# Linear attention with an MLP behind it: first batch's diagonal sums by matrix products, v's odd heads exchanged on chip, 16-bit sign copy, one wide product of U and x

## The chip, the cores and the metric

The kernel runs on one core of a Trainium2 chip. The metric is device microseconds of one execution, the median over several runs. A profile of one execution gives each engine's instructions: TensorE (PE; its weight loads are shown apart as PEld), VectorE (DVE), ScalarE (ACT), GpSimd (POOL) and SyncE (SP), the last of which here only issues DMAs; ACT issues a few too.

## The reference

Two stages, one behind the other. The first is an attention with a decaying state, over B = 4 batches, H = 8 heads, S = 768 positions and D = 48 channels; the second is a low-rank mixing over positions and an MLP.

```python
for t in range(S):
    kt, vt, rt = (k[:, :, t], v[:, :, t], r[:, :, t])
    cur = np.einsum('bhd,bhe->bhde', u[None] * kt, vt)
    y[:, :, t] = np.einsum('bhd,bhde->bhe', rt, state + cur)
    state = w[None, :, :, None] * state + np.einsum('bhd,bhe->bhde', kt, vt)
...
x = y.transpose(0, 2, 1, 3).reshape(B, S, H * D)          # 384 channels
h = x.transpose(0, 2, 1) @ U @ V                          # rank 32
u_ = x + h.transpose(0, 2, 1)
out = u_ + np.maximum(u_ @ w_ch1, 0.0) @ w_ch2            # 384 -> 1536 -> 384
```

The term with u touches only position t itself: it gives v[t] times the number sum over d of r[t,d] u[d] k[t,d], one number for each head and position. These are the diagonal sums. U, V, w_ch1 and w_ch2 come as 64-bit floats, r, k, v, w and u as 32-bit ones.

## The kernel before

**Attention.** Each batch is cut into six chunks of 128 positions (NCH = 6; chunk n counts on over the batches, and `front(n)` is true for the first batch's six). A chunk has two halves of 64 positions and four pairs of heads. Tables of powers of w turn the decay into scaled copies of r and k: `tables` makes them at the start, `tab` among them, which ACT copies from PSUM (L462) once PE has turned it (L460). For a chunk, `a_load` brings r, k and v (L618), and `a_load_odd` brings the odd heads of v a second time, with the two halves of positions exchanged, as `vsw` (L630): TensorE needs an operand's rows to stand where the other operand's rows stand. `a_ks` multiplies k by `tab` (L662), with a memset of the padding columns on POOL (L661). `a_tr` turns r and the scaled k on TensorE (ptr and ptk, L712) and writes rT and kT (L721, L727, L733). `a_part` issues the products: scores (L751), state updates (L766), scores times v (L787), state times r (L793). One chunk's two parts each carry the scores of the next chunk in turn with their own products.

**Diagonal sums.** `a_dv` multiplies r by k (L669) and by u (L671), for the first batch's chunks 1 to 5 on POOL, chunk 0 on whichever of POOL and DVE the planner picks; u lies in `ub`, broadcast to all partitions (L416). `a_dg` sums over d on DVE (L677) and multiplies v by the sums, eight small ACT products in the first batch (L681). `a_x` adds this to the chunk's result (L892).

**Weights.** `weight_units` has 27 units: U, two of V, 12 of w_ch1, 12 of w_ch2 (128 x 384 values each). A unit's 64-bit values become 32-bit floats in four steps: one byte of the low word to a 3-bit number (L518 on DVE or L522 on ACT), a scaling of the high word on ACT (L534), the sign taken over from the high word (L525, DVE), and a shift and join (L528, DVE). A weight is then split into a rounded value (L548, ACT) and the rest (L549, DVE or POOL).

**From attention to MLP.** `c_gx` multiplies U with a chunk's x (three products of 128 columns, L938; they stand in the bank named wake); `c_g0` takes the sum (L947, L948); `c_x` and `c_xu` turn x and add the mixing; then `m_1` and `m_2` are the MLP, in blocks of 384 positions, each hidden tile followed by ACT (L1080) and DVE (L1081). The second to fourth batch's attention runs between the MLP products of the batch before. TensorE's calls through the helper `whole` all show as L344.

**Order.** Nothing is issued in the order of the text. Every step is put in a list with a key (`at(t, ...)`), and a planner, `Plan.schedule`, goes through the operations with an estimated duration each, gives each to one of the engines that it may run on (`one_of`, `on_either`), and fixes the order of each engine's queue. A smaller key goes first among operations that are ready. On the chip every queue keeps that order, and waits where an estimate was wrong. Where the planner sees PE idle before the first batch's U products are done, it puts in products of the identity with itself (wake), which nobody reads. Buffers with a tag (`xbuf`, `wbuf`, `bank`) are rings; the bank ring "acc" has three PSUM banks.

Of the kernel before, what the change touches and what calls it, by code (L numbers as in the profile page):

```python
# [275 lines left out]
def dve(n):  # L276
    return 130 + 1.09 * n


def act(n):  # L280
    return 285 + 0.6 * n
# [7 lines left out]
def rwkv_moe(ctx: ExitStack, tc: tile.TileContext, r, k, v, w, u, U, V, w1, w2, out):  # L289
# [33 lines left out]
    def cbuf(shape, dt, name):  # L323
        return Buf(const, shape, dt, None, 1, name)
# [61 lines left out]

    wT = cbuf([PD, NP, 1], F32, "wT")
    ub = cbuf([128, H, D], F32, "ub")
    flag = cbuf([1, 1], I32, "flag")

    tabT = cbuf([PD, 2, NP, C2 + 2], F32, "tabT")
# [14 lines left out]
            awake.append(bank_)  # L406
        return fn

    def load_w():
        dma(lambda q: q.dma_start(wT.t[:HP, :, 0], bass.AP(tensor=w.tensor, offset=w.offset, ap=[[1, HP], [2 * D, NP]])),  # L410
            [(wT, 0)], [], HP * NP, 4, ns=730)
        dma(lambda q: q.dma_start(wT.t[HP:, :, 0], bass.AP(tensor=w.tensor, offset=w.offset + D, ap=[[1, D], [2 * D, NP]])),
            [(wT, 1)], [], D * NP, 4, ns=580)

    def load_ub():
        dma(lambda q: q.dma_start(ub.t, u.rearrange("h d -> (h d)").partition_broadcast(128)), [ub], [], 128, 1536, ns=650)  # L416
# [70 lines left out]
    def unit(name, shape, parts, split):  # L487

        P_ = shape[0]
        n = 1  # L490
        for s_ in shape[1:]:
            n *= s_
        raw = big([128, 2 * n], I32, f"raw_{name}") if wide else big([128, n], F32, f"raw_{name}")

        def view(ap):
            return ap if len(shape) == 2 else ap.rearrange("p (a c) -> p a c", a=shape[1])

        loaded = [(raw, i) for i in range(len(parts))]
# [12 lines left out]
        def fl():  # L511
            return view(word(0).bitcast(F32) if wide else raw.t[:P_])

        def on_dve_byte():
            nc.vector.tensor_scalar(word(0), byte(), 2.0 ** -5, 7.0, ALU.mult, ALU.min)  # L518

        def on_act_byte():  # L520

            nc.scalar.activation(word(0), byte(), AF.Copy, scale=7.49 / 255)  # L522

        def sign():
            nc.vector.scalar_tensor_tensor(word(0), word(1), -2 ** 31, word(0), ALU.bitwise_and, ALU.bitwise_or)  # L525

        def join():
            nc.vector.scalar_tensor_tensor(word(0), word(1), 3, word(0), ALU.logical_shift_left, ALU.bitwise_or)  # L528

        def convert():  # L530
            if wide:
                op("DVE", 100 + 0.65 * n, on_dve_byte, [(raw, "lo")], loaded, lock=True,
                   alt=[("ACT", act(n) + 100, on_act_byte, False)])
                on_act(n, lambda: nc.scalar.activation(word(1).bitcast(F32), word(1).bitcast(F32), AF.Copy,  # L534
                                                       scale=2.0 ** -112), [(raw, "hi")], loaded)
                op("DVE", dve(n), sign, [(raw, "lo")], [(raw, "hi")], lock=True)
                op("DVE", dve(n), join, [(raw, "lo")], [(raw, "hi")], lock=True)
            split(fl, raw)
        return load, convert
# [45 lines left out]
    def front(n):  # L585

        return n < NCH
# [5 lines left out]
    def a_load(n):  # L593
        b, c = divmod(n, NCH)
        if n < 4:
            t3 = xbuf([128, 2 * H * HP + DM], F32, "uTl" if n % 2 else "uTh", 2, f"ld_{n}")

            def part(i):
                if i < 2:
                    return t3.t[:, i * H * HP:(i + 1) * H * HP].rearrange("p (h d) -> p h d", h=H)  # L600
                return t3.t[:, 2 * H * HP:].rearrange("p (h d) -> p h d", h=H)
            ts = [(t3, i) for i in range(3)]
        else:
            t3 = [wbuf([128, H, D if i == 2 else HP], F32, ("ldr", "ldk", "ldv")[i], (NR, NR, 3)[i],
                       f"ld{'rkv'[i]}_{n}") for i in range(3)]

            def part(i):
                return t3[i].t
            ts = t3
        if turned(n) and not front(n):  # L610
            for i in range(2):
                op("POOL", 250, lambda i=i: nc.gpsimd.memset(part(i)[:, :, D:], 0.0), [(ts[i], f"pad{i}")], [])
        if front(n):
            for i in range(2):
                on_dve(32, lambda e, i=i: e.memset(part(i)[:, :, D:], 0.0), [(ts[i] if n >= 4 else t3, f"pad{i}")], [])
        for i, src in enumerate((r, k, v)):
            eng = "ACT" if n < 3 and i == 1 else "SP"
            dma(lambda q, i=i, src=src: q.dma_start(part(i)[:, :, :D], src[b, :, c * C:(c + 1) * C, :].rearrange("h p d -> p h d")),  # L618
                [ts[i] if n < 4 else (t3, i)] if n < 4 else [(ts[i], "d")], [], 1024, 192, eng=eng)
        rs[n], ks_[n], vs[n] = [((lambda i=i: part(i)), ([(t3, i), (t3, f"pad{i}")] if n < 4 else [(ts[i], "d"), (ts[i], f"pad{i}")])) for i in range(3)]  # L620
        if n < 4 or not front(n):
            a_load_odd(n)

    def a_load_odd(n, dk=0.0):

        b, c = divmod(n, NCH)
        t = (xbuf([128, NP, D], F32, "x", NX, f"vsw_{n}") if front(n) else wbuf([128, NP, D], F32, "vsw", 3, f"vsw_{n}"))
        for i in range(2):
            s0 = c * C + i * C2
            dma(lambda q, i=i, s0=s0: q.dma_start(t.t[(1 - i) * C2:(2 - i) * C2],  # L630
                                                  v[b, 1::2, s0:s0 + C2, :].rearrange("h p d -> p h d")),
                [(t, i)], [], 256, 192, ns=610, eng="ACT" if n < 3 else "SP", dk=dk)
        vsw[n] = t

    bls = {}

# [26 lines left out]
                  only="DVE" if front(n) else None)  # L663

    def a_dv(n):
        (rt, rb), (kt, kb) = rs[n], ks_[n]
        dv = dvs[n] = (xbuf([128, H, D], F32, "hh", NH, f"dv_{n}") if front(n) else
                       wbuf([128, H, D], F32, "dv", 2, f"dv_{n}"))
        on_either(384, lambda e: e.tensor_mul(dv.t, rt()[:, :, :D], kt()[:, :, :D]), [dv], rb + kb,  # L669
                  only="POOL" if front(n) and n else None)  # L670
        on_either(384, lambda e: e.tensor_mul(dv.t, dv.t, ub.t), [dv], [ub], only="POOL" if front(n) and n else None)  # L671

    def a_dg(n):
        dv = dvs[n]
        vt, vb = vs[n]
        dg = dgs[n] = wbuf([128, H], F32, "dg", 2, f"dg_{n}")
# [2 lines left out]
        def small(h0=0, h1=H):  # L679
            for h in range(h0, h1):  # L680
                nc.scalar.activation(dv.t[:, h], vt()[:, h], AF.Copy, scale=dg.t[:, h:h + 1])  # L681
        if front(n):
            for h in range(0, H, 2):
                op("ACT", 560, lambda h=h: small(h, h + 2), [(dv, h)], vb + [dg])
            return
# [248 lines left out]

    def c_gx(n):

        for i in range(3):
            o = pe(225, lambda i=i: whole(wk.t[:3 * R, 128 * (i + 1):128 * (i + 2)], lhsT=Uf.t[:, n].rearrange("p k r -> p (k r)"),  # L938
                                      rhs=xs[n].t[:, 128 * i:128 * (i + 1)], start=False, stop=n == NCH - 1,
                                      skip_group_check=True), [(wk, "g")], [Uf, xs[n]])  # L940
        return o

    def c_g0():
        def pt():
# [278 lines left out]
    at(-100, load_w)  # L1223
    at(-99, lambda: a_load(0))
    at(-98, load_ub)
    at(-97, tables)
    for n in range(1, NCH):
        at(-90 + n, lambda n=n: a_load(n))
    wu = weight_units()
# [9 lines left out]
    for i, (load, convert) in enumerate(wu):  # L1239

        at(-84.9 + 0.01 * i if i < 3 else -50 + 0.1 * i if i < 20 else T0 + 2 * (i - 20), load)
        at(T0 + (use[i] * PER if i > 2 else -14) - 6 + 0.01 * i, convert)

    def prepare(n, t):
        fs = [lambda: a_ks(n), lambda: a_tr(n, 1), lambda: a_tr(n, 0), lambda: a_dv(n)]
        for i, f in enumerate(fs[1:3] + fs[:1] + fs[3:] if n == 0 else fs):
            at(t + 0.2 * i, f)

    def attention(b, t0, per, lead, step):
        n0 = b * NCH  # L1250
        for c in range(NCH):
# [4 lines left out]
                at(t - 1, lambda n=n: a_first(n))  # L1256
            at(t, lambda n=n: a_part(n, 0))
            at(t + per / 2, lambda n=n: a_part(n, 1))
            if front(n + 4):

                at(t + per / 2 + 0.01, lambda n=n: a_load_odd(n + 4, -100.0))
            at(t - 0.1, lambda n=n: a_dg(n))
            if b == 0:
                at(max(t + per - 0.05, 27.0 + 0.1 * c), lambda n=n: gx.append(c_gx(n)))
# [80 lines left out]
```

## Time and profile before

| What | Value |
|---|---|
| median of 3 runs | 438.04 us (437.14 to 439.49) |
| profiled execution | 439.95 us |
| its span, first to last instruction | 437.9 us |
| mean granted TensorE clock | 0.984 |
| busy share PE, PEld, DVE, ACT, POOL | 96%, 91%, 61%, 33%, 13% |
| first product of the MLP | 56.20 us from the span's start |
| DMA | 43.93 MB, 100 GB/s on average |

How the profile is read: a row of a timeline gives start, duration, engine, line, operation, the tiles by name (output <- inputs) and the shapes; what stands in brackets is the time for which the engine was idle before, and what released it. A row of a group gives the count, the busy time, the mean of one in ns, and the idle time before them. Engines overlap their own neighbouring instructions by some tens of ns, so two starts can lie closer than a duration. The granted clock is the share of full speed that TensorE was given.

### The profile page before, as it was taken

The numbers are of one execution on the slowest core, as the hardware profiler recorded it, in microseconds if no ns is written. First come the engines' busy times: TensorE is split into PE (matmuls) and PEld (weight loads), VectorE is DVE, ScalarE is ACT, GpSimd is POOL, SyncE is SP. The second block draws the span as 40 slices with busy tenths as digits, with TensorE's granted clock in tenths as the row PEclk, the third lists the DMA queues.
The fourth block names the chain that finished last, engine by engine and source line by source line (L and its number), as shares of the span: only waits on it lengthen the run. The fifth ranks groups of instructions, "written<-read, shape, count | busy, mean of one in ns | idle before, by whom it ended". The sixth has DMA issues, their size and how long they took to land.

```text
span 437.9 us, 12193 instructions
## 1 busy us (share of the span) xinstructions
PE 419.4 (96%) x5125; PEld 399.8 (91%) x5125; DVE 267.8 (61%) x602; ACT 142.9 (33%) x399; POOL 55.6 (13%) x92
## 2 busy tenths in 40 slices
PE   8889999999999999999999999999999999999991
PEld 8678899889999999999999999999999999999991
DVE  6979699999887757767775456567522351122121
ACT  1679679934421213121112221222112131111110
POOL 2651151223110002011100001101100000000000
PEclk9989699999999999999999999999999999999998
DMA  9979999654466876744586653231100510001001
GB/s 145 162 162 340 335 199 222 103 84 83 81 88 139 148 146 117 136 87 76 105 168 102 96 147 56 48 64 30 55 2 1 98 65 1 0 0 55 1 0 61
DMA packets 178975, 43.93 MB, mean 100 GB/s; under 512 B 168993, under 2 KB 175650, under 8 KB 178914
## 3 DMA queue, kind: packets, MB, share of 16 engines
q1 hardware_dynamic: 174162, 42.20, 46.9%
q10 hardware_dynamic: 4752, 0.89, 1.5%
q8 instruction: 42, 0.69, 0.7%
q14 instruction: 19, 0.16, 0.1%
HBM read 36.57 MB, written 6.49 MB: 98 GB/s over the span
## 4 chain that ended last, share of the span: by engine, by line
PE 81%; DVE 8%; ACT 3%; DMA 3%; POOL 1%; issue 1%; SPq 0%; ACTq 0%; DVEq 0%; POOLq 0%
PE p L344 64%; PE pav L787 5%; PE pav L793 4%; PE pu L344 3%; DVE raw_w L528 2%; DVE raw_w L525 2%; PE pab L751 2%; DMA ld<-in_r_dram 1%; DMA ld<-in_v_dram 1%; PE pab L766 1%; PE wake L344 1%; DVE hl L1081 1%; PE pG L958 1%; ACT dv L681 1%; POOL dv L671 1%
## 5 line engine op out<-in xcount | busy, mean ns | idle before, releaser
L344 PE MATMUL p<-uTh,w1s 128*128 128x384 f32 x576 | 148.2, 338 | 0.0
L1081 DVE SCALAR_TENSOR_TENSOR hl<-p,hh 128x384 fp32r<-128x384 f32 x96 | 53.2, 554 | 119.3 <-ACT hh L1080 119.0
L344 PE MATMUL p<-w2s,hh 128*128 128x384 f32 x576 | 120.3, 340 | 0.6 <-ACT hh L1080 0.6
L1080 ACT ACTIVATE hh<-p 128x384 fp32r<-128x384 f32 x96 | 47.2, 491 | 210.3 <-PE p L344 208.7
L344 PEld LDWEIGHTS p<-uTh,w1s 128*128 128x128 f32 x576 | 102.9, 188 | 0.8
L344 PEld LDWEIGHTS p<-w2s,hh 128*128 128x128 f32 x576 | 99.8, 188 | 2.8 <-ACT hh L1080 0.9
L344 PE MATMUL p<-uTl,w1s 128*128 128x384 f32 x288 | 96.4, 335 | 0.0
L344 PE MATMUL p<-w2s,hl 128*128 128x384 f32 x288 | 65.8, 335 | 0.0
L344 PEld LDWEIGHTS p<-uTl,w1s 128*128 128x128 f32 x288 | 54.0, 188 | 0.0
L344 PEld LDWEIGHTS p<-w2s,hl 128*128 128x128 f32 x288 | 51.4, 188 | 0.0
L787 PE MATMUL pav<-vsw,am 64*64 64x48 f32 x384 | 33.0, 226 | 0.6 <-DVE am L885 0.5
L793 PE MATMUL pav<-S,rT 48*64 48x48 f32 x704 | 32.0, 222 | 0.9 <-issue 0.9
L787 PEld LDWEIGHTS pav<-vsw,am 64*64 64x64 f32 x384 | 26.7, 137 | 6.1 <-issue 4.1
L751 PE MATMUL pab<-rT,kT 48*64 48x64 f32 x768 | 31.2, 228 | 0.3 <-DVE rT L721 0.2
L793 PEld LDWEIGHTS pav<-S,rT 48*64 48x64 f32 x704 | 27.9, 139 | 1.0 <-issue 1.0
L751 PEld LDWEIGHTS pab<-rT,kT 48*64 48x64 f32 x768 | 25.1, 137 | 1.5 <-DVE rT L721 0.5
L787 PE MATMUL pav<-ldv,am 64*64 64x48 f32 x320 | 26.5, 222 | 0.0
L787 PEld LDWEIGHTS pav<-ldv,am 64*64 64x64 f32 x320 | 21.5, 134 | 4.7 <-issue 3.9
L885 DVE TENSOR_TENSOR am<-pab,mask 128x256 f32<-128x256 f32 x48 | 19.7, 417 | 6.8 <-PE pav L793 6.2
L661 POOL MEMSET ks<- 128x128 f32 x24 | 4.9, 205 | 133.2 <-PE pab L766 66.8
L766 PE MATMUL pab<-ldv,ks 64*48 64x48 f32 (+1 forms) x576 | 21.0, 212 | 0.0
L926 ACT ACTIVATE SW<-S,wm 112x48 f32<-112x48 f32 x48 | 12.2, 324 | 21.3 <-DVE S L913 20.0
(127 smaller groups left out, 515.5 us busy)
## 6 DMA issues: line engine op xcount, KB each, us to landing
raw_w<-in_moe_w_ch_dram SPq DMA_DIRECT2D x24, 384.0 KB, 7.4
out_dram<-x SPq DMA_DIRECT2D x24, 192.0 KB, 2.0
ldr<-in_r_dram SPq DMA_DIRECT2D x20, 192.0 KB, 3.3
ldk<-in_k_dram SPq DMA_DIRECT2D x20, 192.0 KB, 3.6
ldv<-in_v_dram SPq DMA_DIRECT2D x20, 192.0 KB, 3.6
bl<-in_r_dram SPq DMA_DIRECT2D x79, 48.0 KB, 2.6
bl<-in_k_dram SPq DMA_DIRECT2D x79, 48.0 KB, 2.5
vsw<-in_v_dram SPq DMA_DIRECT2D x42, 48.0 KB, 3.2
```

The source lines that it names most:

```text
L344: return nc.tensor.matmul(*args, **kw)
L525: nc.vector.scalar_tensor_tensor(word(0), word(1), -2 ** 31, word(0), ALU.bitwise_and, ALU.bitwise_or)
L528: nc.vector.scalar_tensor_tensor(word(0), word(1), 3, word(0), ALU.logical_shift_left, ALU.bitwise_or)
L661: op("POOL", 250, lambda: nc.gpsimd.memset(ks.t[:, :, D:], 0.0), [(ks, "pad")], [])
L751: return [lambda q=q, i=i: nc.tensor.matmul(pt.t[(i ^ j) * C2:(i ^ j) * C2 + C2, q * C2:(q + 1) * C2], lhsT=kT.t[rows, q, i * C2:(i + 1) * ...
L766: return nc.tensor.matmul(pt.t[j * HP:j * HP + m, SU + q * D:SU + (q + 1) * D], lhsT=ks.t[half, 2 * q + j, :m], rhs=vt()[half, 2 * q + j, ...
L787: return nc.tensor.matmul(to(q, j, i), lhsT=am[j].t[half, q, :], rhs=vsw[n].t[half, q, :] if j else vt()[half, 2 * q, :], start=(row == RO ...
L793: return nc.tensor.matmul(to(q, row, i), lhsT=rT.t[rows, q, i * C2:(i + 1) * C2], rhs=St[n, i].t[rows, q, :], start=False, stop=(row == RO ...
L885: on_dve(256, lambda e: e.tensor_tensor(am.t, abs_[n][j].t[:, :SU].rearrange("p (h t) -> p h t", h=NP), mask_.unsqueeze(1).broadcast_to([1 ...
L926: nc.scalar.activation(dec.t[:, q], new.t[:, q], AF.Copy, scale=wm.t[:, q])
L1080: on_act(384, lambda: nc.scalar.activation(hh.t, pt.t[:, :TB], AF.Relu), [hh], [pt])
L1081: on_dve(384, lambda e: e.scalar_tensor_tensor(hl.t, pt.t[:, :TB], 0.0, f32(hh.t), ALU.max, ALU.subtract), [hl], [pt, hh])
```

## The change

It has six parts, the first, third and fourth for the first batch only.

1. `a_dv` and the old `a_dg` go for the first batch. `a_dg_by_pe` takes rT and kT, which are there already for the scores, multiplies them (`rk`, 512 columns, POOL or DVE), and lets TensorE sum over d: for each pair of heads a product of `rk` with two columns, u times w for one head of the pair and for the other (`uw`; w makes up for the scaling in rT and kT). ACT copies the eight sums, and v is multiplied by them in one DVE product or eight ACT ones.
2. The weights' signs (all 27 units): the low word is handled as two 16-bit halves. The byte goes to the lower half, and the sign is a one-source operation from the high word's upper half to the low word's upper half.
3. `vsw` is no longer loaded a second time: `a_odd` copies it from v on ACT or POOL, each half to the other half's partitions.
4. `c_gx` is one product of 384 columns instead of three of 128.
5. u is loaded by columns (`u_cols`) on ACT's queue early; its broadcast `ub` goes to key 0, behind the first 20 weight units.
6. The two units of V are converted at later keys (six us later).

```diff
-    def load_w():
+    def load_cols(t, src, eng="SP"):
...
+    def u_by_w():
+        op("POOL", 300, lambda: nc.gpsimd.memset(uw.t, 0.0), [uw], [])
+        for j in range(2):
+            on_dve(4, lambda e, j=j: e.tensor_mul(uw.t[head_rows(j), :, j:j + 1], ucols.t[head_rows(j)], wT.t[head_rows(j)]),
+                   [uw], [ucols, wT])
...
+        def half(i):
+            return raw.t[:P_].bitcast(U16).rearrange("p (n e) -> p n e", e=4)[:, :, i]
...
-            nc.vector.tensor_scalar(word(0), byte(), 2.0 ** -5, 7.0, ALU.mult, ALU.min)
+            nc.vector.tensor_scalar(half(0), byte(), 2.0 ** -5, 7.0, ALU.mult, ALU.min)
...
-            nc.scalar.activation(word(0), byte(), AF.Copy, scale=7.49 / 255)
+            nc.scalar.activation(half(0), byte(), AF.Copy, scale=7.49 / 255)
...
-            nc.vector.scalar_tensor_tensor(word(0), word(1), -2 ** 31, word(0), ALU.bitwise_and, ALU.bitwise_or)
+            nc.vector.tensor_scalar(half(1), half(3), 0x8000, None, ALU.bitwise_and)
...
-                op("DVE", dve(n), sign, [(raw, "lo")], [(raw, "hi")], lock=True)
+                op("DVE", 100 + 0.65 * n, sign, [(raw, "lo")], [(raw, "hi")], lock=True)
...
+    def a_odd(n):
+        if not front(n):
+            return
+        vt, vb = vs[n]
+        t = vsw[n] = xbuf([128, NP, D], F32, "x", NX, f"vsw_{n}")
+        def half(i):
+            to = t.t[(1 - i) * C2:(2 - i) * C2]
+            return to, vt()[i * C2:(i + 1) * C2].rearrange("p (q j) d -> p q j d", j=2)[:, :, 1]
+        for i in range(2):
+            one_of([("ACT", act(NP * D), lambda i=i: nc.scalar.copy(*half(i)), False),
+                    ("POOL", pool(NP * D), lambda i=i: nc.gpsimd.tensor_copy(*half(i)), True)], [(t, i)], vb)
...
+    def a_dg_by_pe(n):
+        rT, kT = trs[n]
+        vt, vb = vs[n]
+        rk = xbuf([PD, NP, C], F32, "bl", 5, f"rk_{n}")
+        on_either(512, lambda e: e.tensor_mul(rk.t, rT.t[:PD], kT.t[:PD]), [rk], [rT, kT])
+        pt = bank("acc", f"pdg_{n}")
+        def sums():
+            for q in range(NP):
+                whole(pt.t[:, 2 * q:2 * q + 2], lhsT=rk.t[:, q], rhs=uw.t[:, q], start=True, stop=True)
+        pe(DGS, sums, [pt], [rk, uw])
+        dg = dgs[n] = wbuf([128, H], F32, "dg", 2, f"dg_{n}")
+        on_act(H, lambda: nc.scalar.copy(dg.t, pt.t[:, :H]), [dg], [pt])
+        dv = dvs[n] = xbuf([128, H, D], F32, "hh", NH, f"dv_{n}")
+        def small():
+            for h in range(H):
+                nc.scalar.activation(dv.t[:, h], vt()[:, h], AF.Copy, scale=dg.t[:, h:h + 1])
+        one_of([("DVE", dve(384), lambda: nc.vector.tensor_mul(dv.t, vt(), dg.t.unsqueeze(2).broadcast_to([128, H, D])), True),
+                ("ACT", 2000, small, False)], [dv], vb + [dg])
+
+    DGS = 700
...
-        for i in range(3):
-            o = pe(225, lambda i=i: whole(wk.t[:3 * R, 128 * (i + 1):128 * (i + 2)], lhsT=Uf.t[:, n].rearrange("p k r -> p (k r)"),
-                                      rhs=xs[n].t[:, 128 * i:128 * (i + 1)], start=False, stop=n == NCH - 1,
-                                      skip_group_check=True), [(wk, "g")], [Uf, xs[n]])
-        return o
+        return pe(655, lambda: whole(wk.t[:3 * R, 128:], lhsT=Uf.t[:, n].rearrange("p k r -> p (k r)"), rhs=xs[n].t,
+                                     start=False, stop=n == NCH - 1, skip_group_check=True), [(wk, "g")], [Uf, xs[n]])
...
-    at(-98, load_ub)
+    at(-97.5, lambda: load_cols(ucols, u, "ACT"))
     at(-97, tables)
+    at(-96, u_by_w)
+    at(0, load_ub)
...
-        at(T0 + (use[i] * PER if i > 2 else -14) - 6 + 0.01 * i, convert)
+        at(T0 + (use[i] * PER if i > 2 else (-14, -8, -7.9)[i]) - 6 + 0.01 * i, convert)
...
-        fs = [lambda: a_ks(n), lambda: a_tr(n, 1), lambda: a_tr(n, 0), lambda: a_dv(n)]
+        fs = [lambda: a_ks(n), lambda: a_tr(n, 1), lambda: a_tr(n, 0), lambda: a_dv(n), lambda: a_odd(n)]
...
-            if front(n + 4):
-
-                at(t + per / 2 + 0.01, lambda n=n: a_load_odd(n + 4, -100.0))
```

More of the change, by code (lines that the diff above doesn't have):

```diff
@@ L388, in rwkv_moe @@
     ub = cbuf([128, H, D], F32, "ub")
+    ucols = xbuf([PD, NP, 1], F32, "hl", NH, "u_cols")
+    uw = xbuf([PD, NP, 2], F32, "hl", NH, "uw")
     flag = cbuf([1, 1], I32, "flag")
@@ L407, in waking @@
         return fn
-    def load_w():
[L410 to L413, printed above, removed]
+    def load_cols(t, src, eng="SP"):
+        dma(lambda q: q.dma_start(t.t[:HP, :, 0], bass.AP(tensor=src.tensor, offset=src.offset, ap=[[1, HP], [2 * D, NP]])),
+            [(t, 0)], [], HP * NP, 4, ns=730, eng=eng)
+        dma(lambda q: q.dma_start(t.t[HP:, :, 0], bass.AP(tensor=src.tensor, offset=src.offset + D, ap=[[1, D], [2 * D, NP]])),
+            [(t, 1)], [], D * NP, 4, ns=580, eng=eng)
+    def u_by_w():
[3 more added lines that the diff above has]
+                   [uw], [ucols, wT])
     def load_ub():
@@ L620, in a_load, with a_load_odd @@
         rs[n], ks_[n], vs[n] = [((lambda i=i: part(i)), ([(t3, i), (t3, f"pad{i}")] if n < 4 else [(ts[i], "d"), (ts[i], f"pad{i}")])) for i in range(3)]
-        if n < 4 or not front(n):
-            a_load_odd(n)
-    def a_load_odd(n, dk=0.0):
+        a_load_odd(n)
+    def a_load_odd(n):
+        if front(n):
+            return
         b, c = divmod(n, NCH)
-        t = (xbuf([128, NP, D], F32, "x", NX, f"vsw_{n}") if front(n) else wbuf([128, NP, D], F32, "vsw", 3, f"vsw_{n}"))
+        t = vsw[n] = wbuf([128, NP, D], F32, "vsw", 3, f"vsw_{n}")
         for i in range(2):
@@ L631, in a_load_odd @@
                                                   v[b, 1::2, s0:s0 + C2, :].rearrange("h p d -> p h d")),
-                [(t, i)], [], 256, 192, ns=610, eng="ACT" if n < 3 else "SP", dk=dk)
-        vsw[n] = t
+                [(t, i)], [], 256, 192, ns=610)
+    def a_odd(n):
+        if not front(n):
+            return
+        vt, vb = vs[n]
[6 more added lines that the diff above has]
+                    ("POOL", pool(NP * D), lambda i=i: nc.gpsimd.tensor_copy(*half(i)), True)], [(t, i)], vb)
     bls = {}
@@ L665, in a_dv @@
     def a_dv(n):
+        if front(n):
+            return
         (rt, rb), (kt, kb) = rs[n], ks_[n]
[L667 to L671, printed above, removed]
+        dv = dvs[n] = wbuf([128, H, D], F32, "dv", 2, f"dv_{n}")
+        on_either(384, lambda e: e.tensor_mul(dv.t, rt()[:, :, :D], kt()[:, :, :D]), [dv], rb + kb)
+        on_either(384, lambda e: e.tensor_mul(dv.t, dv.t, ub.t), [dv], [ub])
+    def a_dg_by_pe(n):
[17 more added lines that the diff above has]
+    DGS = 700
     def a_dg(n):
+        if front(n):
+            a_dg_by_pe(n)
+            return
         dv = dvs[n]
@@ L681, in small @@
                 nc.scalar.activation(dv.t[:, h], vt()[:, h], AF.Copy, scale=dg.t[:, h:h + 1])
[L682 to L685, printed above, removed]
         one_of([("ACT", 1900, small, False),
@@ L1222, in rwkv_moe @@
     at(-101, lambda: ends.append(pe(230, fill, [wk], [])))
-    at(-100, load_w)
+    at(-100, lambda: load_cols(wT, w))
     at(-99, lambda: a_load(0))
-    at(-98, load_ub)
+    at(-97.5, lambda: load_cols(ucols, u, "ACT"))
     at(-97, tables)
+    at(-96, u_by_w)
+    at(0, load_ub)
     for n in range(1, NCH):
```

## The prediction

> **What bounds the kernel now.** I read the page's busy shares first, then a table of stretches, the chain of waits, and the timelines of the first 60 us. The page says that TensorE (PE) is the bound over most of the run:
>
> ```profile
> span 437.9 us, 12193 instructions
> PE 419.4 (96%) x5125; PEld 399.8 (91%) x5125; DVE 267.8 (61%) x602; ACT 142.9 (33%) x399; POOL 55.6 (13%) x92
> PEclk9989699999999999999999999999999999999998
> ```
>
> The average hides two stages, so I cut the span up. Columns: stretch, length, then busy time (and instructions) of each engine, granted clock, DMA share, GB/s.
>
> ```profile
> core 0: us, PE busy (x) PEld busy (x) DVE busy (x) ACT busy (x) POOL busy (x), PEclk, DMA share, GB/s
> 13.60:17.00 3.40, 2.19 (x40) 1.84 (x41) 3.40 (x9) 2.79 (x13) 1.88 (x3) 1.00 1.21 162
> 23.80:27.20 3.40, 1.41 (x12) 1.05 (x10) 2.51 (x7) 3.23 (x15) 2.65 (x4) 1.00 0.66 123
> 27.20:30.60 3.40, 3.40 (x92) 2.89 (x94) 1.37 (x5) 2.65 (x12) 2.16 (x3) 0.55 1.09 236
> 44.20:47.60 3.40, 2.50 (x45) 2.06 (x44) 2.38 (x6) 1.94 (x6) 0.54 (x1) 1.00 1.02 394
> 47.60:51.00 3.40, 3.40 (x41) 3.31 (x42) 2.47 (x6) 2.63 (x6) 0.00 (x0) 0.57 1.03 395
> 51.00:54.40 3.40, 3.40 (x18) 3.40 (x17) 1.59 (x4) 1.62 (x4) 0.62 (x1) 0.50 0.97 220
> ...
> 60.00:70.00 10.00, 9.38 (x53) 8.83 (x52) 9.84 (x19) 8.43 (x24) 2.33 (x2) 1.00 0.85 229
> 80.00:90.00 10.00, 9.32 (x113) 8.28 (x112) 10.00 (x21) 7.95 (x20) 2.47 (x4) 1.00 0.73 116
> 90.00:100.00 10.00, 9.24 (x151) 8.45 (x151) 9.97 (x24) 4.33 (x11) 2.54 (x4) 1.00 0.50 83
> 100.00:400.00 300.00, 300.00 (x3633) 287.70 (x3633) 173.84 (x389) 67.94 (x186) 22.07 (x37) 1.00 0.42 79
> ```
>
> From 100 to 400 us PE has no gap and the full clock: nothing in the change touches that work, so it is a block of fixed length. What can move is when it starts (the first product of the MLP, at 56.20) and the small gaps between 60 and 100, where VectorE (DVE) is full and PE misses 0.62, 0.68 and 0.76 us, 2.06 together.
>
> ```profile
> 56.20 0.60 PE L344 MATMUL p<-uTh,w1s 128*128 128x384 f32 x2
> ...
> 56.81 0.51 PE L344 MATMUL p<-uTh,w1s 128*128 128x384 f32 x2
> 57.16 0.33 PE L344 MATMUL p<-uTl,w1s 128*128 128x384 f32 x1
> ```
>
> So the question is what the first batch's six chunks cost before 56.20. The timelines show where PE or DVE stood still there, each with its releaser in brackets:
>
> ```profile
> 8.98 0.60 PE L460 MATMUL pt_tab<-ident,tw 112*128 112x112 f32 x4
> 13.13 0.63 PE L712 MATMUL ptk<-ident,ks 128*128 128x128 f32 x4 [0.70 <-DVE ks L662]
> 15.85 0.63 PE L712 MATMUL ptk<-ident,ks 128*128 128x128 f32 x4 [1.21 <-DVE ks L662]
> 26.45 0.66 PE L712 MATMUL ptk<-ident,ks 128*128 128x128 f32 x4 [1.99 <-POOL ks L661]
> 31.47 0.71 PE L344 MATMUL wake<-ident 128*128 128x128 f32 x4
> ```
>
> ```profile
> 8.32 2.10 ACTq L630 DMA_DIRECT2D vsw<-in_v_dram  x2
> 10.46 0.48 ACT L462 COPY tab<-pt_tab 128x384 f32<-128x384 f32 x1 [6.95 <-DMA vsw<-in_v_dram]
> ```
>
> ```profile
> 17.68 0.55 DVE L677 TENSOR_REDUCE dg<-dv 128x8 f32<-128x384 f32 x1 [0.65 <-POOL dv L671]
> ```
>
> ```profile
> 24.72 1.53 POOL L671 TENSOR_TENSOR dv<-dv,ub 128x384 f32<-128x384 f32 x1
> 26.19 0.20 POOL L661 MEMSET ks<- 128x128 f32 x1
> ```
>
> All of this hangs on the old diagonal sums and on v's second load. A 0.2 us memset of a padding column stands in GpSimd's (POOL's) queue behind the product r·k·u and stops PE for 1.99 us; the copy of tab is ready when L460 ends at 9.58 and goes at 10.46, because ScalarE (ACT) is still issuing v's second copy.
>
> **The change, part by part.** Durations of what goes, and of the nearest thing to what comes, are in these group rows (count, busy us, mean ns) and tile rows (shortest, median, longest ns):
>
> ```profile
> L671 POOL TENSOR_TENSOR dv<-dv,ub 128x384 f32<-128x384 f32 x6 | 6.6, 1107 | 8.2 <-DVE kT L721 7.9
> L681 ACT ACTIVATE dv<-ld,dg 128x48 f32<-128x48 f32 x32 | 7.6, 328 | 2.5 <-DVE dg L677 2.5
> L721 DVE TENSOR_TENSOR rT<-ptr,tabT 112x512 f32<-112x512 f32 x6 | 4.1, 679 | 0.0
> L677 DVE TENSOR_REDUCE dg<-dv 128x8 f32<-128x384 f32 x6 | 3.3, 543 | 1.5 <-POOL dv L671 1.5
> L892 DVE TENSOR_TENSOR x<-pav,dv 128x384 f32<-128x384 f32 x6 | 3.3, 549 | 0.9 <-PE pav L793 0.9
> L922 POOL TENSOR_TENSOR SW<-S,wm 112x192 f32<-112x192 f32 x4 | 2.0, 509 | 0.9 <-DVE S L913 0.9
> ```
>
> ```profile
> L525 DVE SCALAR_TENSOR_TENSOR raw_w<-raw_w x24: 544/548/1427, 40.0 to 96.0; 128x384 int32<-128x384 int32 x24
> L518 DVE TENSOR_SCALAR raw_w<-raw_w x1: 352/352/352, 39.8 to 39.8; 128x384 int32<-128x384 uint8 x1
> ```
>
> Removed per chunk: two products on POOL (mean 1.1 us; chunk 0's first is on DVE), a reduction of 0.54 on DVE, eight small products of 0.33 on ACT, and v's two loads of 48 KB (64 positions of 4 heads, 192 bytes each). Added per chunk: one product rT·kT of 512 columns (0.68 on DVE by L721, or 1107 x 512/384 = 1.48 on POOL), four PE products with two columns each, an ACT copy of eight columns, one DVE product (0.55 by L892) or eight small ACT ones, and two ACT or POOL copies of half of v (0.51 by L922 on POOL). Of 2.2 on POOL, 0.54 on DVE and 2.6 on ACT, at most 1.5, 1.2 and 1.5 come back, never all at once. The relief is large, and PE pays for it.
>
> *Start, to 18 us.* ACT's copy of tab no longer waits for L630: -0.9, shared by ks and the chunk-1 transposes at 13.13 and 15.85. DVE is full in 13.6:17.0 and loses two reductions (1.1) and the 0.65 wait at 17.68, and gains up to two products of 0.68 and two of 0.55. The strided load of u goes on ACT's queue ahead of chunk 1's k, in the place of two vsw issues, and has until the tables are done: 0. I take -1.5; bounds 0 (DVE gets all that is new) and -2.7 (the three terms together).
>
> *The stall at 26.45.* The memset still stands in POOL's queue, but behind one product, of operands that are already made, or behind none: -2.0, bounds 0 and -2.0. The clock of 0.55 in 27.2:30.6 follows a stretch with 1.41 us of PE work; with the hole filled the lost 3.4 x 0.45 = 1.5 goes too: -1.5, bounds 0 and -1.5.
>
> *Sums on PE.* The nearest row is the products with the identity at 43.16, in which each fp32 product is two instructions with a new weight tile each:
>
> ```profile
> 43.16 1.38 PE L344 MATMUL pu<-ident,x 128*128 128x128 f32 x10
> 35.76 2.21 PE L344 MATMUL wake<-x,Uf 128*96 128x128 f32 x18 [0.16 <-ACT Uf L554]
> ```
>
> That is 0.13 an instruction, so four sums are eight instructions and 1.05 us, if a new weight tile costs the same with two columns as with 128; 6.3 for six chunks. The first three fall into the 0.70, 1.21 and other holes before 26, where PE is not the bound; the last three are 3.15 less the filler at 31.47 (0.71): +2.5. Bounds: 0 (all in holes) and +6.3.
>
> *x for the wide product.* Now 18 instructions in 2.21, 0.123 each, six per chunk: 0.74. After: two instructions of 384 columns. If time goes by columns, nothing changes; if, like the MLP's of 384 columns, each takes (57.16 - 56.81)/2 = 0.175, 0.39 a chunk is saved, 2.3 in all. The 128-column fp32 row is dearer per column than that, so I stay near the first: -0.2, bounds 0 and -2.3.
>
> *Signs by halves.* L525 (548) becomes a one-source operation, nearest to L518 (352): 0.2 x 24 = 4.8 us of DVE, over a stage in which DVE is full and PE misses 2.06. Most of those gaps end on products of the second batch's attention that queue on DVE, so I take -0.8; bounds 0 and -2.0. It could also cost: L518 is one record. Were it no cheaper than L525, that term is 0.
>
> *V's conversion moved later.* PE waited 0.43 for the conversion of U at 33.77 (the row below); V's now comes after the attention's own work, and must be there for the last products before 56.20: -0.4, bounds -0.5 and +1.0.
>
> ```profile
> 33.77 0.38 PE L712 MATMUL ptk<-ident,ks 128*128 128x128 f32 x2 [0.43 <-DVE raw_u L525]
> ```
>
> *Loads.* u's broadcast goes behind the weights on the SyncE (SP) queue; its first reader is now the second batch: 0. Without v's second copy the weights are asked for sooner: 0 on PE's path, since at 56.20 none is missing.
>
> *Tail.* Two stretches at 0.57 and 0.50 before the MLP cost 3.4 x 0.43 + 3.4 x 0.50 = 3.2. They follow 44.2:47.6 with 0.9 idle. The same tail remains (last x, wide product, copy, products), arriving elsewhere: half of it, -1.6, bounds 0 and -3.2.
>
> Sum: -1.5 - 2.0 - 1.5 + 2.5 - 0.2 - 0.8 - 0.4 - 1.6 = -5.5. The profiled execution took 439.95 us with the span of 437.9, so 2.05 lies around it; it is 1.9 above the median of the runs, 438.04 (437.14 to 439.49). By the profiled execution 434.45, by the median 432.5. Around 0.5% (2.2 us) is what a measurement of this kernel can tell from no change.
>
> **The rivals.**
>
> *A: the front closes up (faster still).* If the tail's clock stays full (-3.2) and the sums hide in holes (+1.0 instead of +2.5) and the wide product saves 1.0, the sum is -9.4: 428.6. For: every one of these holes is named above with a cause that the change removes or softens. Against: the order of every queue is fixed beforehand from estimated times, so holes appear wherever an estimate is wrong.
>
> *B: PE waits for the product rT·kT.* The sums stand in PE's in-order queue, with the next transposes and parts behind them. If the product is on POOL and is drawn out as L671 was (1.53 once, the other five 1.0 each by the group row), PE waits 0.5 a chunk, and the add into x behind the copy and product again as long: 6 x 0.7 = 4.2, leaving -1.3: 436.7. For: POOL's and DVE's queues are the place of every stall above. Against: chunk 1's parts began 4.25 us after chunk 0's, by the two rows below, and rT and kT are made about one chunk ahead, so the new chain of 1.48 + 1.05 + 0.55 and an ACT copy has that long.
>
> ```profile
> 16.40 0.31 PE L787 MATMUL pav<-vsw,am 64*64 64x48 f32 x2
> ...
> 20.65 0.31 PE L787 MATMUL pav<-vsw,am 64*64 64x48 f32 x2
> ```
>
> *C: the clock (slower).* Half clock came after stretches with little work in the array, and 47.6:51.0, in which PE is recorded busy throughout, was followed by one at 0.50: recorded busy time is not what holds the clock. Two-column products are nearly all weight loading. If the front, whose holes are now filled by such products and not by the 128-column filler, loses three stretches more than before (3 x 1.7 = 5.1) and keeps the three it has (1.5 + 1.6 not gained), the sum is -5.5 + 3.1 + 5.1 = +2.7: 440.7. It decides from the third further stretch on. Against: 13.6:17.0 with 2.19 us busy was followed by full clock.
>
> The Trainium skill ("TensorE: Matmul & The Clock Gate", Part 1) says that the clock halves after an idle window of about 3.4 us and comes back after a busy one. By that rule no hole here (at most 2.0 us) would halve it, the sum would lack its two clock terms (-5.5 + 3.1 = -2.4, 435.6), and C could not happen. The stretches at 0.55, 0.57 and 0.50 speak against that: this clock fell without such an idle window.
>
> *D: the parts do not act* (the new operations are placed so that each replaces an equal wait): 438.
>
> **How the numbers follow.** Main case 0.55 at 432.5, its own range 429.5 to 435.8; A 0.18; B 0.13, three quarters of it within 0.5%; C 0.11; D 0.03. Faster by over 0.5% (below 435.85): 0.53 + 0.18 + 0.03 = 0.74. Within: 0.02 + 0.10 + 0.03 = 0.15, slower 0.11. The range reaches into A and over B and D: 426.5 to 438.8, which leaves out most of C and the far end of A.
>
> **What would show it.** Right: no wait of PE for POOL near 24 to 26 us; tab copied directly after L460; PE's first MLP product at 50 to 52 instead of 56.20; sums of about 1.05 a chunk; the sign operation near 0.35; PE's gaps in the 40 us after the MLP starts below 2.0. Wrong: the first MLP product later than 54, clock digits below 9 in more than three stretches of 3.4 us, sums that end on a wait for rk, or a longer PE gap in the MLP for want of weights, which would mean that DVE and not the front sets its start.

## The result and the profile after

The changed kernel takes 448.68 us (median of 4 runs, 448.03 to 448.78) against 438.76 before: a ratio of 1.0237 (95% interval 1.0203 to 1.0271). The forecast was 432.5 with a range of 426.5 to 438.8; the time went the other way.

The page after, in the lines that answer to those of before (span, busy shares, granted clock in 40 slices):

```profile
span 446.2 us, 12160 instructions
PE 425.1 (95%) x5137; PEld 402.3 (90%) x5137; DVE 271.9 (61%) x612; ACT 142.1 (32%) x345; POOL 45.4 (10%) x87
PEclk9978599999999999999999999999999999999998
```

POOL is 10 us lighter, as meant. ACT is not, although the old sums' small products are gone: something took their place. The stretches after (columns as in the prediction):

```profile
27.20:30.60 3.40, 2.12 (x68) 2.03 (x68) 2.68 (x9) 2.52 (x5) 0.20 (x1) 0.76 0.87 205
30.60:34.00 3.40, 3.40 (x12) 2.38 (x11) 3.40 (x9) 3.34 (x7) 0.85 (x3) 0.50 1.00 378
34.00:37.40 3.40, 3.40 (x84) 1.95 (x86) 1.32 (x5) 2.50 (x6) 0.39 (x1) 0.73 1.02 392
...
44.20:47.60 3.40, 3.05 (x66) 2.98 (x68) 2.87 (x7) 3.35 (x7) 1.30 (x2) 0.77 1.08 352
47.60:51.00 3.40, 3.40 (x36) 2.18 (x34) 2.45 (x5) 2.87 (x7) 0.70 (x1) 0.50 0.68 134
51.00:54.40 3.40, 3.40 (x40) 3.31 (x37) 2.65 (x5) 2.70 (x6) 1.75 (x2) 0.50 0.88 196
54.40:57.80 3.40, 3.40 (x20) 3.11 (x20) 3.22 (x7) 2.72 (x5) 1.72 (x3) 0.72 1.04 239
...
80.00:90.00 10.00, 7.17 (x43) 6.49 (x42) 9.58 (x21) 7.70 (x18) 1.42 (x2) 1.00 0.35 53
90.00:100.00 10.00, 8.10 (x104) 6.77 (x102) 9.35 (x18) 3.60 (x7) 2.97 (x5) 1.00 0.58 98
```

Two things to see. The clock is below 0.8 in seven of these stretches of 3.4 us, where before had three. And between 80 and 100 us PE now misses 2.83 and 1.90 us, where it missed 0.68 and 0.76. The timelines of PE and DVE after give the start of the MLP and two of the holes:

```profile
28.48 0.25 PE L835 MATMUL pav<-ld,am 64*64 64x48 f32 x1 [1.68 <-DVE seen L914]
...
60.95 0.60 PE L344 MATMUL p<-uTh,w1s 128*128 128x384 f32 x2
...
87.61 0.66 PE L760 MATMUL ptr<-ident,ldr 128*128 128x128 f32 x4 [2.37 <-ACT kT L775]
```

```profile
27.86 0.38 DVE L530 TENSOR_SCALAR raw_u<-raw_u 128x192 uint16<-128x192 uint8 x1 [1.83 <-DMA raw_u<-in_moe_U_dram]
28.27 0.16 DVE L914 COPY seen<-pav 1x1 f32<-1x1 f32 x1
```

The MLP starts 4.75 us later (60.95 against 56.20), and the span ends 8.3 later, so the rest was lost behind it. At 28 us the attention's small copy stands in DVE's queue behind U's conversion, which waits for U's load, and PE waits 1.68 us for that copy. The conversion's rows after, one tile, shortest/median/longest ns:

```profile
L534 ACT ACTIVATE raw_w<-raw_w x24: 1029/1086/1150, 31.0 to 82.5; 128x384 uint16<-128x384 uint8 x24
```

```profile
L537 DVE TENSOR_SCALAR raw_w<-raw_w x24: 586/631/1403, 40.4 to 94.5; 128x384 uint16<-128x384 uint16 x24
```

The byte on ACT (L534 after, L522 before) reads the same bytes and now stores 16 bits instead of 32. Before it was:

```profile
L522 ACT ACTIVATE raw_w<-raw_w x23: 535/562/629, 39.0 to 84.0; 128x384 int32<-128x384 uint8 x23
```

It nearly doubled. The sign on DVE is 631 where the old two-source operation took 548 and the forecast said 352.

### The profile page after: what moved, and what is told of

It reads as the page before. It is cut to its first block, busy times and chain, and to the rows that moved or that the text cites. A ratio compares the mean times of both kernels' runs of the same rounds, so it can differ in the third digit from the quotient of the medians.

```text
span 446.2 us, 12160 instructions
## 1 busy us (share of the span) xinstructions
PE 425.1 (95%) x5137; PEld 402.3 (90%) x5137; DVE 271.9 (61%) x612; ACT 142.1 (32%) x345; POOL 45.4 (10%) x87
## 4 chain that ended last, share of the span: by engine, by line
PE 78%; DVE 7%; ACT 5%; SPq 4%; DMA 3%; issue 1%; ACTq 0%
PE p L344 61%; PE pav L835 5%; SPq L630 4%; PE pav L841 3%; PE pu L344 3%; ACT raw_w L534 2%; DVE raw_w L537 2%; PE pab L799 2%; DMA raw_u<-in_moe_U_dram 1%; PE wake L344 1%; PE pab L814 1%; DVE raw_w L540 1%; ACT raw_w L546 1%; DMA ub<-ud 1%; DVE w2s L561 1%; DVE hl L1126 1%
## 5 line engine op out<-in xcount | busy, mean ns | idle before, releaser
L835 PE MATMUL pav<-vsw,am 64*64 64x48 f32 x384 | 34.1, 229 | 0.5 <-DVE am L933 0.5
L835 PEld LDWEIGHTS pav<-ldv,am 64*64 64x64 f32 x320 | 22.4, 138 | 6.9 <-issue 3.9
L835 PE MATMUL pav<-ldv,am 64*64 64x48 f32 x320 | 27.5, 227 | 1.2 <-ACT seen L914 1.2
L534 ACT ACTIVATE raw_w<-raw_w 128x384 uint16<-128x384 uint8 x24 | 26.1, 1086 | 0.0
```

Source lines behind the costliest of these rows:

```text
L534: nc.scalar.activation(half(0), byte(), AF.Copy, scale=7.49 / 255)
L835: return nc.tensor.matmul(to(q, j, i), lhsT=am[j].t[half, q, :], rhs=vsw[n].t[half, q, :] if j else vt()[half, 2 * q, :], start=(row == RO ...
```

## The experiments

Theory 1 was that the 16-bit stores are the loss; theory 2 that the sums on PE, with the clock that falls in the front, are. "First MLP" is the start of the MLP's first product in the profiled execution; "clock lost" is the sum of (1 - granted clock) x 2 us over stretches of 2 us in the first 72 us there; "waits" are PE's waits from the first MLP product to 130 us, added up. A ratio is to runs of before that were made along with the kernel's own (their medians lie between 437.89 and 438.76), so ratios compare two rows better than medians do.

| Kernel | median us (runs) | ratio to before (95%) | first MLP | clock lost | waits |
|---|---|---|---|---|---|
| before | 438.76 (4) | 1 | 56.20 | 5.1 | 1.9 |
| after | 448.68 (4) | 1.0237 (1.0203 to 1.0271) | 60.95 | 8.5 | 5.1 |
| e1_words | 443.89 (4) | 1.0123 (1.0099 to 1.0147) | 61.54 | 11.9 | 1.8 |
| e2_halves_only | 443.85 (4) | 1.0137 (1.0115 to 1.0159) | 55.62 | 3.4 | 4.5 |
| e3_byte_word | 446.28 (4) | 1.0180 (1.0155 to 1.0205) | 61.29 | 8.5 | 3.3 |
| e4_words_oldsums | 440.24 (5) | 1.0058 (1.0032 to 1.0085) | 56.89 | 3.4 | 3.6 |
| e5_words_pad | 438.80 (10) | 1.0025 (0.9996 to 1.0055) | 52.81 | 0.0 | 2.7 |
| e6_oldsums_vload | 436.36 (10) | 0.9960 (0.9933 to 0.9987) | 52.61 | 0.0 | 3.4 |
| e7_oldsums_three | 442.49 (4) | 1.0088 (1.0058 to 1.0119) | 59.70 | 5.1 | 2.3 |
| e8_oldsums_vkeys | 442.80 (4) | 1.0094 (1.0063 to 1.0124) | 56.86 | 5.1 | 4.1 |
| e9_after_pad | 448.19 (4) | 1.0226 (1.0187 to 1.0265) | 61.02 | 6.8 | 4.1 |
| e10_pad_vload | 439.79 (12) | 1.0028 (1.0006 to 1.0051) | 59.18 | 5.1 | 1.8 |
| e12_pad_byte_word | 443.12 (4) | 1.0120 (1.0083 to 1.0158) | 57.59 | 1.7 | 3.2 |
| e14_pad_u_act | 447.02 (4) | 1.0207 (1.0170 to 1.0244) | 58.44 | 1.7 | 4.1 |
| e15_words_vload | 444.03 (4) | 1.0123 (1.0099 to 1.0147) | 61.34 | 8.6 | 2.0 |

One profiled execution is one draw: where a kernel's runs lie far apart (e10: 437.04 to 443.54, and the profile was the one of 443.54), its clock column isn't the median's. The profile of e5 is the fastest of its ten runs (437.09), that of e1 the slowest of its four (444.62). The column also ends at 72 us: between 72 and 104 us, e2 lost 3.4 us more, and e9, e10, e14 and e15 1.7 each.

The mean granted clock of every run is on record, too. The part of the span that it took away, (1 - clock) x span, is on average 5.3 us for before (50 runs made beside the kernels of the table, without one of 806.27 us), 11.6 after, 12.2 for e1, 7.2 for e2, 3.8 for e5, 2.7 for e6, 4.4 for e10 and 10.1 for e15. It includes the half clock of the last few us of each span, and it is an upper estimate of what the clock cost: where PE would have waited anyway, it cost less.

**Whole words (e1).** The halves undone in the changed kernel:

```diff
-            nc.scalar.activation(half(0), byte(), AF.Copy, scale=7.49 / 255)
+            nc.scalar.activation(word(0), byte(), AF.Copy, scale=7.49 / 255)
-            nc.vector.tensor_scalar(half(1), half(3), 0x8000, None, ALU.bitwise_and)
+            nc.vector.scalar_tensor_tensor(word(0), word(1), -2 ** 31, word(0), ALU.bitwise_and, ALU.bitwise_or)
```

(DVE's byte and the sign's estimate likewise.)

> The changed kernel with the weights' signs and bytes back on whole 32-bit words (that part undone, all else kept). Theory 1, the 16-bit stores are the loss (in the profile after, the byte on ACT went from 562 to 1086 ns in the median, the sign on DVE from 548 to 631 instead of 352): the byte is back at about 560 ns, the MLP starts at 50 to 54 us and the time is 430 to 437, below the 438.8 before. Theory 2, the sums on PE and the half clock that follows in the front are the loss, and the stores hide in idle time of ACT: 444 to 448, first MLP product still after 58 us.

443.89: at the lower edge of theory 2's range, and the MLP starts no earlier (61.54), as theory 2 has it. But the halves are half of the loss (4.8 us), and PE's waits in the MLP fall from 5.1 to 1.8, while the clock lost does not fall (12.2 against 11.6 over all runs). Neither theory alone holds.

**Halves alone (e2).** The same lines the other way round, in the kernel before.

> The kernel before with the 16-bit halves alone. Theory 1: slower than before by 3 to 10 us (24 x 0.52 us more on ACT and 24 x 0.08 on DVE, in a stage that is full), 442 to 449. Theory 2: within 2 us of before, 437 to 441.

443.85, 5.8 above the 438.07 of before that was run beside it: theory 1 as far as the halves go. They act more through gaps than through the clock: waits in the MLP are 4.5 against 1.9, and over all runs the clock took 1.9 us more than before (7.2 against 5.3). In this kernel, too, the byte and the sign have their new durations (line numbers of e2):

```profile
L525 ACT ACTIVATE raw_w<-raw_w x22: 1032/1079/1120, 39.9 to 83.8; 128x384 uint16<-128x384 uint8 x22
```

```profile
L528 DVE TENSOR_SCALAR raw_w<-raw_w x24: 593/606/1542, 40.3 to 88.4; 128x384 uint16<-128x384 uint16 x24
```

DVE's own byte, too, takes 628 ns with the 16-bit store (two records), where its one record before, from the same input to 32 bits, took 352. The costliest wait of PE there is for DVE, which makes the next chunk's kT late:

```profile
PE ptr L715 <- DVE kT L736: 3.4, 2, 3.2
```

That wait lies in a stretch in which the clock fell as well, behind the 72 us of the table:

```profile
80.00:90.00 10.00, 6.83 (x26) 6.41 (x25) 9.41 (x17) 7.12 (x14) 3.95 (x4) 0.66 0.33 52
```

**Byte as a word, sign by halves (e3).**

> The changed kernel with the byte stored as a whole 32-bit word again, the sign still from half to half. Tells ACT's store from DVE's. Theory 1 with ACT's store as the cause: within 2 us of the kernel with whole words throughout, 431 to 438. If DVE's sign (estimated at 350 ns, measured 631) counts as much: 440 to 445. Theory 2: 444 to 448.

446.28: 2.4 from ACT's byte (448.68 to 446.28) and 2.4 from DVE's sign (to 443.89). Both count, the sign as much as the byte, though it is only 0.08 us longer in the median than what it replaced, and over all 27 units DVE spent 18.2 us on it in e3's profile and 17.7 in e1's. DVE's time alone does not explain 2.4 us. The planner's estimate, 350 ns where 631 were measured, orders a full queue wrongly and may be the rest; e11 was to test that, and does not settle it.

**Old sums (e4).** The old `a_dv`, `a_dg` and load of u in e1; wide product, exchange and V's keys stay.

> Whole words, and the old diagonal sums (POOL products, DVE reduction, eight ACT products) in the changed kernel; v exchanged on chip, the wide product and V's later conversion stay. It weighs the sums on PE. Theory 1, in which the sums on PE relieve the other engines: slower than the same kernel with sums on PE by 1 to 5 us. Theory 2, in which the sums are the loss: faster than it by 3 us or more.

440.24, 3.65 faster than e1: theory 2. The clock lost is 3.4 instead of 11.9. That is the first sign of what the sums do, and e5 tests it.

**Padding the sums (e5).** In e1, u times w gets 126 columns of zeros behind its two, so that a sum streams 128 columns:

```diff
-    uw = xbuf([PD, NP, 2], F32, "hl", NH, "uw")
+    uw = xbuf([PD, NP, 128], F32, "bl", 5, "uw")
-                whole(pt.t[:, 2 * q:2 * q + 2], lhsT=rk.t[:, q], rhs=uw.t[:, q], start=True, stop=True)
+                whole(pt.t[:, 128 * q:128 * q + 128], lhsT=rk.t[:, q], rhs=uw.t[:, q], start=True, stop=True)
```

(the copy of the sums picks the two columns out). The order of every engine's queue is the same but for one memset.

> Whole words, sums on PE, with the two columns of u times w padded by zeros to 128, so that each sum streams 128 columns instead of 2; the padding leaves the sums as they are. Theory C, two-column products give PE's activity too little and the clock falls: fewer stretches at half clock than the seven (17 to 27 us and 44 to 58 us) of the same kernel with two columns, and 438 to 441 us instead of 443.9. Rival, what costs is PE's time in the sums and their waits whatever their width: 443 to 446, with as many stretches at half clock.

438.80, five us faster for more work, as theory C has it. Here is e1, two columns:

```profile
10.20:13.60 3.40, 3.40 (x86) 3.23 (x85) 3.05 (x8) 0.98 (x3) 1.18 (x2) 1.00 1.48 177
13.60:17.00 3.40, 3.00 (x70) 2.60 (x68) 3.12 (x8) 1.27 (x6) 0.51 (x1) 1.00 1.17 142
17.00:20.40 3.40, 3.40 (x65) 3.15 (x63) 2.11 (x7) 1.84 (x6) 0.71 (x2) 0.53 0.94 188
20.40:23.80 3.40, 3.40 (x72) 3.29 (x72) 2.22 (x4) 0.27 (x2) 0.00 (x0) 0.50 0.73 136
```

and e5, 128 columns:

```profile
10.20:13.60 3.40, 3.40 (x85) 3.23 (x85) 2.94 (x7) 0.92 (x3) 1.19 (x2) 1.00 1.48 177
13.60:17.00 3.40, 2.99 (x70) 2.54 (x68) 3.26 (x8) 1.23 (x6) 0.51 (x1) 1.00 1.43 178
17.00:20.40 3.40, 3.26 (x73) 2.79 (x72) 2.79 (x9) 2.14 (x8) 0.71 (x2) 1.00 0.75 145
20.40:23.80 3.40, 3.32 (x135) 3.08 (x136) 3.00 (x9) 0.49 (x3) 0.54 (x2) 1.00 0.98 196
```

Up to 17 us PE and DVE run the same instructions in the same order in both, and PE's recorded busy time from 13.60 to 17.00 is 3.00 and 2.99. Then one falls to half clock and the other does not. What differs is the width of the products. The eight instructions of a chunk's sums take nearly the same time on PE; first e1 at full and at half clock, then e5:

```profile
43.37 0.95 PE L344 MATMUL pdg<-uw,rk 112*128 112x2 f32 x8
20.05 1.70 PE L344 MATMUL pdg<-uw,rk 112*128 112x2 f32 x8
```

```profile
18.96 1.06 PE L344 MATMUL pdg<-uw,rk 112*128 112x128 f32 x8
```

So two columns save a tenth of the time and count less towards the clock. The width is not all that decides. One of e5's ten runs lost the clock too (443.50 at a mean of 0.979). And in the changed kernel, with two-column sums at 13.14, 18.30 and 23.04, the clock stood at 1.00 up to 27.20, behind the same recorded busy time that e1 had:

```profile
13.60:17.00 3.40, 3.00 (x87) 2.43 (x89) 3.12 (x8) 1.00 (x5) 0.51 (x1) 1.00 1.13 135
17.00:20.40 3.40, 3.08 (x102) 2.91 (x97) 2.93 (x8) 1.77 (x7) 0.71 (x2) 1.00 0.90 172
```

The Trainium skill ("TensorE: Matmul & The Clock Gate", Part 1) has a clock that halves after an idle window and returns after a busy one. e1's 20.40:23.80, recorded busy throughout at 0.50, shows that the profile's busy time isn't the activity that decides.

**The other parts, on e4's base.** v's second copy loaded again (e6: `a_load_odd` for every chunk, no `a_odd`), three products for the wide one (e7), V's old keys (e8).

> Whole words, old sums, v's second copy loaded again for all six chunks; left of the change are the wide product and V's later conversion. If the exchange on chip is what leaves 2.2 us against before: 437 to 439. If it helps, as the prediction had it: 441 to 443. If it is neither: 440.

> Whole words, old sums, v exchanged on chip, and x times U again in three products of 128 columns. If the wide product costs (it cannot be split among other work, and its result is one block): 437 to 439. If, as predicted, it saves 0 to 2 us: 440 to 442.

> Whole words, old sums, and V converted at its old keys; v exchanged on chip and the wide product stay. If V's later conversion costs (DVE at 36 to 43 us, and the last products before the MLP wait for it): 437 to 439. If it saves 0.4, as predicted: 440 to 441.

e6 is 436.36, below all three of its forecasts and faster than before. With the exchange, the sums and the halves undone, the wide product and V's later conversion remain, and one thing more: e6 loads all of v's second copies from SP's queue, where the kernel before issues those of the first three chunks from ACT's. These are the rows of before, then that of e6:

```profile
vsw<-in_v_dram SPq DMA_DIRECT2D x42, 48.0 KB, 3.2
vsw<-in_v_dram ACTq DMA_DIRECT2D x6, 48.0 KB, 5.7
```

```profile
vsw<-in_v_dram SPq DMA_DIRECT2D x48, 48.0 KB, 3.3
```

So the 0.4% is the gain of the three together; e10 and e15 have the same loads. e7 and e8 are 2.2 and 2.6 slower than e4 in the median, 0.3% and 0.4% by the ratios, both a little above their forecasts; their runs lie apart from e4's, the intervals do not. Each lost 1.7 us more to the clock in its profile, which is most of it. The exchange looked like 3.9 us here, but e6's profile lost no clock and e4's 3.4, so that was open.

**The exchange at padded sums (e10), padding in the changed kernel (e9), honest estimates (e11).**

> Whole words, padded sums on PE, wide product, V later, and v's second copy loaded instead of exchanged on chip. With both kernels at full clock this shows the exchange by itself. If the exchange costs by its operations, as the step from 440.2 to 436.4 with old sums suggests: 434 to 436.5. If that step was the clock alone (one of the two lost 3.4 us to it): 437.5 to 440, the same as with the exchange.

> The changed kernel whole, 16-bit halves too, with the sums' two columns padded by zeros to 128. If the clock's loss and the halves' loss add up: about 5 us below the changed kernel, 443 to 445, no or one stretch at half clock, and the MLP's gaps still at 4 to 5 us in PE's waits. If the halves alone would leave holes that halve the clock anyway: 446 to 449.

> The changed kernel with the planner told what the halves measured (byte on ACT 1.09 us, on DVE 0.65, sign 0.65). If the loss of the halves comes from queues ordered by estimates that are too low: 444 to 446. If it is the engines' time itself: 447 to 449.

e10 is 439.79 against 438.80 with the exchange: the exchange costs nothing by itself against a load from SP's queue (e1 and e15, below, say the same with two columns: 1.0123 both). e9, 448.19, met its second forecast: padding gained 5.1 with whole words, and with halves 0.5, which the intervals do not tell from nothing. With halves there are holes enough to lose the clock anyway (e9):

```profile
27.20:30.60 3.40, 1.53 (x62) 1.53 (x64) 2.01 (x7) 1.67 (x3) 0.00 (x0) 0.80 0.66 191
30.60:34.00 3.40, 3.40 (x25) 2.67 (x20) 3.38 (x9) 3.34 (x8) 1.06 (x4) 0.70 0.92 318
```

e11 ran at 437.86, 446.76, 447.37 and 449.46, with mean clocks of 0.995, 0.977, 0.974 and 0.967. These lie too far apart for a ratio, and nothing is built on it: whether the estimates or the durations cost is open.

**What keeps the clock down with halves (e12, e14), and the padding again (e15).**

> The changed kernel with padded sums and with the byte stored as a whole word; the sign still from half to half. Both undone (padded, whole words) gave 438.8, padding alone 448.2, the byte's word alone 446.3. If ACT's doubled store is what keeps the padded kernel at half clock: 439 to 442, at most one such stretch. If DVE's sign, or the wait for U's load on DVE, keeps it there: 444 to 447 with the half clock at 28 to 34 us still there.

> The changed kernel with padded sums and halves, U's byte on ACT alone, so that DVE's queue no longer waits for U's load ahead of the attention's small copy (that wait held PE for 2.3 us at 29 us). If that hole starts the half clock at 28 to 34 us: no half clock there and 443 to 446. If it does not: 447 to 449.

> Whole words, two-column sums on PE, v's second copy loaded: the kernel of 439.8 (padded, 12 runs from 437.0 to 443.5) without the padding. If two columns cost the clock wherever the sums stand: 441.5 to 445 with at least two more stretches at half clock in the median. If the five us of padding were special to one order of the queues: 439 to 441.

e12, 443.12, lies between the two: of the 9.4 us from e9 to e5, ACT's byte is 5.1 and DVE's sign 4.3, and the padding is worth 3.2 with one of them left. e14, 447.02, isn't clear of e9: the hole at 29 us went, and PE waited 2.4 us for U's copy and 3.1 for kT instead. e15, 444.03 against e10's 439.79: two columns cost 4.2 us in another order of the queues too, with 8.6 us of clock lost in the profile, and over all runs 10.1 against e10's 4.4.

## Why the prediction was wrong

One part at a time, by ratios: before to e6 (wide product, V later, v's second copy from SP's queue) -0.4%; to e15 (sums on PE) +1.6%; to e1 (exchange) 0.0%; to after (halves) +1.1%; together +2.4%. Point by point:

- **Start, -1.5: right.** tab is copied at 9.50 instead of 10.46, and the first part of chunk 0 begins at 14.48 instead of 16.40.
- **The stall at 26.45, -2.0: right on its cause,** PE no longer waits for POOL there. The third chunk's first part begins at 25.06 instead of 27.25. What was late next was U: a wait of 1.7 us for DVE at 28.48, which I had not looked for when I said that the earlier loads cost nothing on PE's path.
- **Sums, +2.5 with bounds 0 and +6.3: PE's time in them was right** (0.95 a chunk for 1.05), what they cost was not. I priced them as PE time, to be hidden in holes. Their price is that the holes are filled with products that do not hold the clock: +1.6%, some 7 us, from e6 to e15, of which the padding gives back 4.2 us. That is rival C, in mechanism and sign, at a chance of 0.11 and with too small a price, for I gave it nothing else to go wrong beside it. In the changed kernel itself, where the clock first fell at 28 us behind the wait for U, padding alone gave back no more than 0.5.
- **The two clock terms, -1.5 and -1.6: failed.** 8.5 us of clock were lost in the profile after, 5.1 before. The profile of before, from which I read both terms, was one with more to gain than most: its mean clock was 0.984, that of the 50 runs 0.988.
- **"The relief is large": not where it was needed.** All six products rk (0.69) and all six products of v with the sums (0.56) ran on DVE, 7.4 us in all, where 3.8 left it (six reductions and chunk 0's first product). DVE is the engine that is full. This fits the result that with padded sums and whole words (e5) the change gains nothing, 1.0025 (0.9996 to 1.0055), where the sum without the term of the halves was -4.7 us; no run tests it apart.
- **Signs by halves, -0.8 with bounds 0 and -2.0: the single term that failed worst.** It cost 4.8 us (e1 to after), 5.8 alone (e2). I took L518, which stores 32-bit words, as the nearest row for an operation that stores 16-bit ones, and did not price the byte at all, because its code line looked unchanged but for the name of the target. The bound above zero was missing. The Trainium skill ("VectorE: DVE Perf Modes", What auto-detection actually checks) gives a one-source operation between even shapes in SBUF the mode of two elements a cycle. The 631 ns here are longer than the 548 of the two-source operation on as many elements, and do not agree.
- **Wide product -0.2 and V later -0.4: right in sign** by e7 and e8, mostly through the clock, for which neither term had a price. e6's 1.8 us are theirs together with the move of v's loads to SP's queue.
- **Rival B** did not decide: the profile after has no wait of PE for rk, that of e5 one of 0.6 us.
- **Slips of the working** that change little: 1.38/10 is 0.14 an instruction and not 0.13; B's two waits of 0.5 a chunk make 6.0 and not 4.2; and ACT and POOL could each have been given more than the 1.5 that I called the most.

How far the losses can be parted is limited: they aren't additive. Either the halves' holes or the two-column sums suffice to lose the clock, so undoing one alone gains 4.8 (halves) or 0.5 (padding), and both together 9.9.

**What stays open.** Why PE's clock lets go in one stretch and not in its neighbour of the same recorded busy time; why a 16-bit store costs ACT twice a 32-bit one; whether the sign's 2.4 us come from its wrong estimate; and what makes up the 3.4 us that e10, with its padded sums, takes beyond e6, of which the granted clocks of all runs account for some 1.7 (4.4 against 2.7). The version to keep is e6, at 0.996 (0.9933 to 0.9987).

## What to carry to other kernels

Before an engine's work is moved to a matrix unit whose clock can fall, ask what the new products stream: narrow products can fill its time and still let the clock fall. A store's width is part of an operation's price, so look for a row with the same output type before using its duration. Where queues are ordered beforehand by estimates, look out for an operation whose estimate is wrong by a quarter of a microsecond, 24 times over, in a full queue: here that may be what cost 2.4 us, though no run shows it apart. And when work leaves one engine, follow where the planner puts what replaces it.

## What the runs showed of the hardware

- A product of two columns took PE nearly as long as one of 128 columns (0.95 and 1.06 us for eight instructions). With two columns (e1) the granted clock fell to 0.50 for stretches in which PE was recorded busy throughout; with the same queues and 128 columns (e5) the profiled execution kept 1.00 through the first 72 us.
- A byte copied by ACT to 16-bit halves at a pitch of 8 bytes took 1086 ns for 384 elements, to 32-bit words at the same pitch 562; DVE's one-source sign between 16-bit halves took 631; its byte to a 32-bit word took 352, to a 16-bit half 628 (e2).
